# PSUM as one tile of eight named banks, read in pairs, in a kernel of a state-space convolution and a linear attention

## The chip, the cores and the metric

The kernel runs on one core of a Trainium2 chip. A core has a matrix engine (TensorE, PE in the profile, with its weight loads as PEld), a vector engine (VectorE, DVE), a scalar engine (ScalarE, ACT), GpSimd (POOL) and SyncE (SP), which here issues the DMA transfers. Each engine takes its own instructions in the order in which the program gives them, and waits on semaphores for the others. The metric is the time of one execution on the device, in microseconds (us); of several runs the median is taken.

## The reference

Two independent branches whose outputs stand side by side, 2048 x 1152 in fp32.

```python
def _A_ref(u, log_A_real, A_imag, C_real, C_imag, log_dt, D_skip):   # L=2048, D=576, N=128
    dt = jnp.exp(log_dt)
    A = -jnp.exp(log_A_real) + 1j * A_imag
    C = (C_real + 1j * C_imag) * dt[:, None]
    P = jnp.exp((A * dt[:, None])[:, :, None] * pos[None, None, :])
    K = 2.0 * jnp.einsum("dn,dnl->dl", C, P).real
    ...
    y = jnp.fft.irfft(Uf * Kf[None, :, :], L2)[:, :, :L]   # causal convolution of u with K
    ...
    return y + u * D_skip[None, None, :]

def _B_ref(x, wqkv, w_phi, wo):        # S=2048, D=576, 32 heads of 18
    ...
    q, k, v = qkv[0], qkv[1], qkv[2]   # of x @ wqkv
    pq = jnp.einsum("bhsd,hdf->bhsf", q, w_phi)
    pk = jnp.einsum("bhsd,hdf->bhsf", k, w_phi)
    phi_q = jnp.concatenate([_softmax(pq, axis=-1), _softmax(-pq, axis=-1)], axis=-1)
    phi_k = jnp.concatenate([_softmax(pk, axis=-1), _softmax(-pk, axis=-1)], axis=-1)
    kv = jnp.einsum("bhsf,bhsd->bhfd", phi_k, v)
    z  = jnp.einsum("bhsf->bhf", phi_k)
    num = jnp.einsum("bhqf,bhfd->bhqd", phi_q, kv)
    den = jnp.einsum("bhqf,bhf->bhq", phi_q, z)[..., None] + 1e-6
    o = num / den
    return (lambda x, *d: x.transpose(*d))(o, 0, 2, 1, 3).reshape(B, S, D) @ wo
```

## The kernel before

**How it is put together.** `body` does not issue instructions itself. It records some 3000 operations with `Plan.op`: each with its engine, the buffers that it reads and writes, and a function that issues it. A copy with engine `"any"`, and some other operations, have a second engine (`copy`, L265, and `tt`, L273). The order in which all are issued is written out by hand in the string `ORDER`, a list of operation numbers: an `x` behind a number puts that operation on its second engine, and a colon with a number puts so many filler matmuls on zeros ahead of it (`emit`, L194 to L207). So the order on each engine's queue, and on SP's for the transfers, is this string's. `Buf` objects get their memory when the first operation that uses them is issued, from pools with a fixed number of buffers by tag (L256 to L259). All PSUM buffers have the tag `ps`, of which there are 8, one bank (512 fp32 of each partition) each.

**Attention.** Weights of keys and queries are first multiplied by `w_phi` (`fold`, L311). Every gemm takes fp32 numbers as a high and a low part (`hi`, `lo`; fp32r), so one output of 128 rows is 14 matmuls that add up in one bank (`gemm`, from L372). There are 16 tiles of 128 rows. `key_tile` (L434) makes keys and values, 1152 columns, in three gemms of 378, 378 and 396 columns, in the banks `pa`, `pb` and `pc`; `pb` holds the end of the keys and the start of the values. `softmax` (L393) reads the keys from PSUM in two parts, 21 and 11 heads: for each a maximum and a minimum over a head (L400, L401), the addition of the maximum (L282) and a small sum (L403), all on DVE; after that one exponential for both signs on ACT (L408), sums on POOL (L411) and DVE (L412), and the scaling. Values are copied beside ones (`v1`), in two copies. 32 small matmuls of heads then add to `kvt`, one bank that stays taken through the key stage. `query_tile` (L495) makes queries in two gemms of 288 columns (`gemm_halves`, L385), takes `softmax` in two parts of 16 heads, transposes it through PSUM (`turn`, L504), multiplies by the key-value sums and divides (`divide`, L518), transposes again, and multiplies by `wo` in two gemms of 288 columns, copied out by two copies (`ot`).

**Convolution.** The FFT is done by matmuls in two steps with transfers through DRAM between them. `u_first` (L576) does the first step for the input, four banks of 288 columns, four copies to `zi`. The filter is made in 18 pairs of groups (`phases`, `waves`, `group`): `params` (L647) computes for each of 6 blocks of 96 columns, in a chain of 96-wide DVE and ACT operations (L659 and L666 are its helpers), the angles' integer phases `pi`; POOL builds the phases, ACT takes sines, PE and ACT the exponentials of the sizes (L762), DVE multiplies them (L768 to L773), PE sums over states. `k_first` (L787) with `first` (L564) does the first FFT step of the filter. `product` (L827, 16 of them) does the second step of both, multiplies (L282, `ac`), and goes the first step back; `last` (L905, 16) does the last one and writes the output. Each of these writes 288-column results to two or four banks, and copies each bank out by itself (`us`, `zo`, `yo`).

**The order around.** Key tiles are first, with the input's first steps; the groups run from then to about three quarters of the time, with queries and later products beside them; products, queries and last steps fill the end.

Of the kernel before, what the change touches and what calls it, by code (L numbers as in the profile page):

```python
# [11 lines left out]
I32 = mybir.dt.int32  # L12
# [130 lines left out]
class Buf:  # L143


    def __init__(self, tag, shape, dt):
        self.tag, self.shape, self.dt = tag, shape, dt
        self.writers, self.readers, self.left, self.end, self.t = [], [], 0, 0.0, None
# [9 lines left out]
class Plan:  # L158
# [14 lines left out]
    def buf(self, tag, shape, dt=F32):  # L173
        return Buf(tag, shape, dt)
# [19 lines left out]
    def emit(self, k, o, eng, fill=0):  # L194
        for b in o[4]:
            if b.t is None:
                b.t = self.pools[b.tag].tile(b.shape, b.dt, name=b.tag, tag=b.tag)
        if fill:
            b, (rows, cols) = o[11], o[10]
            t = b.t  # L200
# [8 lines left out]
    def run(self):  # L209

        seen = set()
        for word in ORDER.split():
            word, _, fill = word.partition(":")
            k = int(word.rstrip("x"))
# [4 lines left out]
            self.emit(k, o, o[12][0] if word[-1] == "x" else o[0], int(fill or 0))  # L219
# [25 lines left out]
def body(tc, nc, i, out, ctx):  # L245
# [10 lines left out]
    tags({1: "zero ident w1 w3 hp quarter dsk kvb fT wh wl ks E sel dt th cre cim ax ay mx mn ld ldc",  # L256
          2: "v1 o ot pi mg ff ub kb zo us2 ac yo zi", 3: "e fk x9", 4: "cs", 7: "small"})
    tags({8: "ps"}, space=PSUM)
# [52 lines left out]
    def fold(w_t, w, done, stage, after):  # L311
# [4 lines left out]
        def block(g, c, cs):  # L316
            wt, pa, pb = B(stage[g], [128, 640]), B("ps", [128, 4, 126]), B("ps", [128, 126])
            op("sp", c_dma(c * 2560), lambda: sp.dma_start(wt.t[:c], w_t[cs, :]), w=[wt])

            def f():  # L320
                for k in range(4):
                    mm(pa.t[:, k, :c], wt.t[:c, k * 128:k * 128 + 128], phiw.t[:c, g, :c])
            op("pe", 4 * 222, f, r=[wt, phiw], w=[pa], with_=[hi, lo])

            op("pe", 222, lambda: mm(pb.t[:, :c], wt.t[:c, 512:640], phiw.t[:c, g, :c]), r=[wt, phiw], w=[pb], with_=[hi, lo])
            a, b = (lambda x: x.t[:, 0:4, cs]), (lambda x: x.t[:, 4, cs])
            for x, ps, n in ((a, (lambda: pa.t[:, :, :c]), 4 * c), (b, (lambda: pb.t[:, :c]), c)):
                src, half = pa if x is a else pb, Mark()
                op("act", c_act(n), lambda x=x, ps=ps: act.activation(x(hi), ps(), AF.Copy), r=[src], w=[done[g], half], with_=[hi])
                op("dve", c_dve(n), lambda x=x, ps=ps: dve.tensor_tensor(x(lo), ps(), x(hi).bitcast(F32), op=ALU.subtract),  # L330
                   r=[src, half], w=[done[g]], with_=[hi, lo])
# [6 lines left out]
    def whole(src, w, done, stage, eng):  # L338
        hi, lo = w

        def third(c):
            wi, half = B(stage[c], [128, 5, 192]), Mark()
            cs = slice(D + 192 * c, D + 192 * c + 192)
# [49 lines left out]
    def softmax(parts, total=False):  # L393

        rg, sm, e = B("small", [128, 32]), B("small", [128, 32, 2]), B("e", [128, 2, H, DH])

        def part(p, hs, v):
            m = hs.stop - hs.start
            ends = B("small", [128, m, 2])
            op("dve", c_dve(DH * m), lambda: dve.tensor_reduce(ends.t[:, :, 0], v(), axis=AX.X, op=ALU.max, negate=True), r=[p], w=[ends])  # L400
            op("dve", c_dve(DH * m), lambda: dve.tensor_reduce(ends.t[:, :, 1], v(), axis=AX.X, op=ALU.min), r=[p], w=[ends])  # L401
            tt("dve", lambda: e.t[:, 0, hs, :], v, lambda: ends.t[:, :, 0:1].to_broadcast([128, m, DH]), ALU.add, [p, ends], [e], DH * m)
            op("dve", c_dve(2 * m), lambda: dve.tensor_reduce(rg.t[:, hs], ends.t, axis=AX.X, op=ALU.add), r=[ends], w=[rg])  # L403
        for p in parts:
            part(*p)
# [28 lines left out]
    def key_tile(t):  # L434
# [3 lines left out]
        pa, pb, pc = B("ps", [128, 378]), B("ps", [128, 378]), B("ps", [128, 396])  # L438
        by_head = lambda ap: ap.rearrange("p (h f) -> p h f", f=DH)
# [4 lines left out]
        e = softmax([(pa, slice(0, 21), lambda: by_head(pa.t)), (pb, slice(21, 32), lambda: by_head(pb.t[:, 0:198]))])  # L444
# [3 lines left out]
        copy("any", lambda: v1.t[:, 0:10, 0:18], lambda: by_head(pb.t[:, 198:378]), [pb], [v1], 180)  # L448
        copy("any", lambda: v1.t[:, 10:32, 0:18], lambda: by_head(pc.t), [pc], [v1], 396)
# [45 lines left out]
    def query_tile(t):  # L495
# [3 lines left out]
        e = softmax([(ps[c], slice(16 * c, 16 * c + 16), lambda c=c: ps[c].t.rearrange("p (h f) -> p h f", f=DH)) for c in range(2)], True)  # L499
# [4 lines left out]
        def turn(j0, n):  # L504
# [6 lines left out]
            op("pe", 110 * n, f, r=[e, ident], w=[tp], with_=[fT], busy=0.5)  # L511
# [37 lines left out]
        for c, cs in enumerate(halves):  # L549
# [499 lines left out]
```

## Time and profile before

| | us |
|---|---|
| median of 3 runs | 576.01 (573.24 to 577.25) |
| the profiled execution | 574.2 |
| its span, first to last instruction | 572.4 |

The profile is of that one execution. "Busy" is the time in which an engine worked on instructions; a matmul's time runs to the end of its pipeline, so neighbouring matmuls overlap, and PE's busy time holds short stalls. A row with "idle before" tells how long the engine stood still ahead of these instructions, and what ended that. The slices below are 1/40 of the span each, in tenths busy.

```profile
PE   7998799999999999998999999999999999999996
PEld 6998689888977777887887666867878866667884
DVE  5999779989989999999999999999876689866642
ACT  4775857788678989798699968788744334232332
POOL 0736589977778676982569755887311244112110
PEclk7999899999999999999999999999999999999999
DMA  8957432252857685717755758985568899998587
```

### The profile page before, as it was taken

Reading aid. Unit: us, or ns where it says so; the run is one execution under the profiler, and the core shown is the slowest. Engines: PE = TensorE matmul, PEld = TensorE weight load, DVE = VectorE, ACT = ScalarE, POOL = GpSimd, SP = SyncE. Lnnn points to the kernel's source line nnn. Section 1 sums busy time; section 2 is a strip of 40 time slices with the busy share of each in tenths; the row PEclk is TensorE's granted clock in tenths of the full one; section 3 lists DMA queues with packets and bytes.
Section 4 is the critical chain, followed back from the end, with each engine's and each line's share of the span. In section 5 each row is a group of like instructions: output and inputs, shape, how many; then the busy total and the mean of one; then the engine's idle time right before and its main releaser. Section 6 shows DMA issues by size and latency. Waiting matters only on the chain.

```text
span 572.4 us, 18462 instructions
## 1 busy us (share of the span) xinstructions
PE 542.3 (95%) x7526; PEld 444.1 (78%) x7526; DVE 491.0 (86%) x1059; ACT 383.6 (67%) x656; POOL 316.6 (55%) x454
## 2 busy tenths in 40 slices
PE   7998799999999999998999999999999999999996
PEld 6998689888977777887887666867878866667884
DVE  5999779989989999999999999999876689866642
ACT  4775857788678989798699968788744334232332
POOL 0736589977778676982569755887311244112110
PEclk7999899999999999999999999999999999999999
DMA  8957432252857685717755758985568899998587
GB/s 249 302 172 254 159 145 88 86 187 91 277 150 217 205 264 159 208 44 184 216 190 156 239 153 233 309 255 188 169 246 228 228 288 282 286 277 280 172 283 208
DMA packets 91314, 119.22 MB, mean 208 GB/s; under 512 B 9826, under 2 KB 73186, under 8 KB 91230
## 3 DMA queue, kind: packets, MB, share of 16 engines
q1 hardware_dynamic: 91230, 118.04, 67.1%
q8 instruction: 59, 0.97, 0.7%
q14 instruction: 25, 0.20, 0.1%
HBM read 68.76 MB, written 49.26 MB: 206 GB/s over the span
## 4 chain that ended last, share of the span: by engine, by line
PE 48%; DVE 28%; DMA 8%; ACT 7%; issue 4%; POOL 3%; SPq 1%; DVEq 0%; POOLq 0%; ACTq 0%
PE ps L263 44%; DVE cs L768 2%; DVE E L769 2%; PE ps L510 2%; DMA kb<-dram 2%; POOL cs L720 2%; DVE zi L268 2%; DVE e L282 2%; DMA zi<-dram 1%; DVE small L401 1%; DVE small L412 1%; DVE small L400 1%; DVE E L773 1%; ACT ps L762 1%; DVE x L278 1%
## 5 line engine op out<-in xcount | busy, mean ns | idle before, releaser
L263 PE MATMUL ps<-wh,x 128*128 128x288 f32 (+2 forms) x1008 | 241.0, 320 | 2.5 <-DVE zi L268 1.0
L263 PEld LDWEIGHTS ps<-wh,x 128*128 128x128 f32 x1008 | 173.9, 189 | 13.9 <-issue 3.4
L263 PE MATMUL ps<-wl,x 128*128 128x288 f32 (+2 forms) x560 | 175.4, 314 | 0.0
L720 POOL TENSOR_TENSOR cs<-cs,pi 128x32 int32<-128x32 int32 (+4 forms) x180 | 112.0, 627 | 8.7
L263 PEld LDWEIGHTS ps<-wl,x 128*128 128x128 f32 x560 | 106.0, 189 | 0.7
L762 ACT ACTIVATE ps<-ps 128x512 f32<-128x512 f32 x108 | 59.9, 588 | 12.2 <-PE ps L263 11.9
L411 POOL TENSOR_TENSOR o<-e 128x576 f32<-128x576 f32 x32 | 42.1, 1316 | 35.5 <-ACT e L408 35.5
L278 POOL TENSOR_TENSOR e<-e,small 128x576 f32<-128x576 f32 (+1 forms) x27 | 44.9, 1662 | 28.1 <-DVE small L282 23.1
L278 POOL TENSOR_TENSOR ac<-ac 128x288 f32<-128x288 f32 x43 | 34.5, 820 | 45.4 <-DVE ac L282 37.2
L278 POOL TENSOR_TENSOR e<-small,e 128x576 f32<-128x576 f32 x24 | 28.5, 1189 | 42.8 <-DVE small L403 29.3
L768 DVE TENSOR_TENSOR cs<-ps,cs 128x1024 f32<-128x1024 f32 x36 | 43.6, 1212 | 7.4 <-ACT ps L762 7.3
L282 DVE TENSOR_TENSOR ac<-us,ps 128x576 f32<-128x576 f32 x64 | 45.2, 745 | 5.3 <-PE ps L263 4.9
L263 PEld LDWEIGHTS ps<-kvb,fT 126*128 126x128 f32 (+1 forms) x320 | 38.4, 188 | 8.1 <-issue 2.2
L769 DVE TENSOR_TENSOR E<-ps,cs 128x1024 f32<-128x1024 f32 x36 | 43.6, 1211 | 1.0 <-ACT ps L762 1.0
L408 ACT ACTIVATE e<-e 128x1152 f32<-128x1152 f32 x32 | 37.3, 1168 | 9.0 <-POOL e L278 5.3
L263 PEld LDWEIGHTS ps<-E,cs 128*32 128x32 f32 x2304 | 34.3, 110 | 11.4 <-issue 4.4
L263 PE MATMUL ps<-kvb,fT 126*128 126x133 f32 (+1 forms) x320 | 41.5, 280 | 1.2 <-ACT zi L268 1.2
L263 PE MATMUL ps<-sel,mg 128*128 128x512 f32 x108 | 38.1, 444 | 3.8 <-ACT sel L271 2.5
L263 PE MATMUL ps<-E,cs 128*32 128x64 f32 x2304 | 40.2, 221 | 0.9 <-DVE E L769 0.4
L268 ACT ACTIVATE zi<-ps 128x288 f32<-128x288 f32 x77 | 28.0, 411 | 17.2 <-PE ps L263 12.0
L263 PE MATMUL ps<-kb,fk 128*64 128x288 f32 x256 | 36.4, 416 | 2.4 <-DMA kb<-dram 1.2
L744 ACT ACTIVATE cs<-cs 128x1040 f32<-128x1040 int32 x36 | 38.3, 1063 | 0.4 <-POOL cs L739 0.2
(141 smaller groups left out, 1039.7 us busy)
## 6 DMA issues: line engine op xcount, KB each, us to landing
xd<-x SPq DMA_DIRECT2D x16, 576.0 KB
dram<-zi SPq DMA_DIRECT2D x16, 576.0 KB
dram<-zi SPq DMA_DIRECT2D x32, 288.0 KB
x<-xd SPq DMA_DIRECT2D x16, 576.0 KB
kb<-dram SPq DMA_DIRECT2D x32, 288.0 KB
ub<-dram SPq DMA_DIRECT2D x32, 288.0 KB
dram<-zo SPq DMA_DIRECT2D x32, 288.0 KB
zi<-dram SPq DMA_DIRECT2D x16, 576.0 KB
```

The source lines that it names most:

```text
L263: pe.matmul(o, l, r, start=start, stop=stop, skip_group_check=skip)
L268: op(("act", "dve"), (c_act(n), c_dve(n)), lambda e: act.activation(dst(), src(), AF.Copy) if e == "act" else dve.tensor_copy(dst(), src() ...
L278: op(eng, [c_dve(n[0]) if e == "dve" else c_pool(n[1]) for e in eng], lambda e: (dve if e == "dve" else pool).tensor_tensor(dst(), a(), b( ...
L282: op(eng, c_dve(n) if eng == "dve" else c_pool(n), lambda: e.tensor_tensor(dst(), a(), b(), op=alu), r=r, w=w, lock=eng == "pool" or not a ...
L408: op("act", c_act(1152) + 40, lambda: act.activation(e.t, e.t, AF.Exp), r=[e], w=[e], table="exp")
L411: op("pool", c_pool(470), lambda: pool.tensor_tensor(pair.t, e.t[:, :, :, 0:9], e.t[:, :, :, 9:18], op=ALU.add), r=[e], w=[pair], lock=True)
L510: pe.transpose(tp.t[0:m, j - j0, :], e.t[:, sign, 7 * g:7 * g + GRP[g], :].rearrange("p h f -> p (h f)"), ident.t)
L720: op("pool", c_pool(2 * n * W), lambda n=n, j=j: pool.tensor_tensor(x()[:, :, :, n:2 * n], x()[:, :, :, 0:n], pi.t[:, j:j + 2, gs].bitcast ...
L744: act.activation(cs.t[:, 1], cs.t[:, 1].bitcast(I32), AF.Sin, scale=TURN)
L762: op("act", c_act(512), lambda: act.activation(ps.t, ps.t, AF.Exp), r=[ps], w=[ps], table="exp")
L768: op("dve", c_dve(64 * W), lambda: dve.tensor_tensor(F(), both(M.t), F(), op=ALU.mult), r=[M, cs], w=[cs])
L769: op("dve", c_dve(64 * W), lambda: dve.tensor_tensor(E.t[:, :, :, 32:64], both(up.t), cs.t[:, :, :, 0:32], op=ALU.mult), r=[up, cs], w=[E])
```

## The change

PSUM becomes one tile of eight banks. A buffer asks for one bank or two neighbouring ones, and the order string names the first bank of each buffer that an operation takes (`@` and digits) in place of a pool that hands them out. Results that stood in two banks become one buffer over two, and one operation reads both:

- keys are one pair of 2 x 288 columns and values another, four gemms of 288 in place of three; `softmax` reads the keys, or queries, in one part;
- `v1`, `ot`, `zi`, `us`, `zo` and `yo` are copied in pairs, and `ac` is one multiplication of 4 x 288 in place of two;
- `params` runs its chain on 192 columns, for two blocks at a time, and only the last steps on each block;
- `yo` uses the buffers of `ot` (three instead of two each), `mx` that of `ax`;
- `fold` puts its five results into one pair;
- operations are renumbered (2575 in place of 2973) and the order string is new, with 38 filler matmuls where there were 62, and other choices of the second engine in places.

```diff
+    def banks(self, b, k):
+        p, *dims = b.shape
+        t = self.psum[0:p, k:k + b.banks]
...
-    def emit(self, k, o, eng, fill=0):
+    def emit(self, k, o, eng, fill=0, at=""):
+        at = iter(at)
         for b in o[4]:
-            if b.t is None:
+            if b.t is None and b.tag == "ps":
+                self.banks(b, int(next(at)))
+            elif b.t is None:
                 b.t = self.pools[b.tag].tile(b.shape, b.dt, name=b.tag, tag=b.tag)
...
-          2: "v1 o ot pi mg ff ub kb zo us2 ac yo zi", 3: "e fk x9", 4: "cs", 7: "small"})
-    tags({8: "ps"}, space=PSUM)
+          2: "v1 o pi mg ff ub kb zo us2 ac zi", 3: "e fk x9 ot", 4: "cs", 7: "small"})
+    pl.psum = ctx.enter_context(tc.tile_pool(name="banks", bufs=1, space=PSUM)).tile([128, 8, 512], F32, name="psum")
...
     def gemm_halves(x, w, done, c0):
-        r = []
-        for cs, need in zip(halves, done):
-            ps = B("ps", [128, 288])
-            gemm(x, w, need, ps, lambda ps=ps: ps.t, slice(c0 + cs.start, c0 + cs.stop))
-            r.append(ps)
-        return r
+        ps = B("ps", [128, 2, 288], banks=2)
+        for c, (cs, need) in enumerate(zip(halves, done)):
+            gemm(x, w, need, ps, lambda c=c: ps.t[:, c], slice(c0 + cs.start, c0 + cs.stop))
+        return ps
...
-        def part(p, hs, v):
-            m = hs.stop - hs.start
-            ends = B("small", [128, m, 2])
-            op("dve", c_dve(DH * m), lambda: dve.tensor_reduce(ends.t[:, :, 0], v(), axis=AX.X, op=ALU.max, negate=True), r=[p], w=[ends])
...
-        for p in parts:
-            part(*p)
+        ends, two = B("small", [128, H, 2]), lambda ap: ap.rearrange("p (c h) -> p c h", c=2)
+        op("dve", c_dve(D), lambda: dve.tensor_reduce(two(ends.t[:, :, 0]), v(), axis=AX.X, op=ALU.max, negate=True), r=[p], w=[ends])
+        op("dve", c_dve(D), lambda: dve.tensor_reduce(two(ends.t[:, :, 1]), v(), axis=AX.X, op=ALU.min), r=[p], w=[ends])
...
-        pa, pb, pc = B("ps", [128, 378]), B("ps", [128, 378]), B("ps", [128, 396])
-        gemm(x, wkv, have_k[0:3], pa, lambda: pa.t, slice(0, 378))
-        gemm(x, wkv, have_k[3:5] + have_v[0:1], pb, lambda: pb.t, slice(378, 756))
-        gemm(x, wkv, have_v, pc, lambda: pc.t, slice(756, 1152))
+        pk = gemm_halves(x, wkv, (have_k[0:3], have_k[2:5]), 0)
+        pc = gemm_halves(x, wkv, (have_v[0:2], have_v[1:3]), D)
...
-        copy("any", lambda: v1.t[:, 0:10, 0:18], lambda: by_head(pb.t[:, 198:378]), [pb], [v1], 180)
-        copy("any", lambda: v1.t[:, 10:32, 0:18], lambda: by_head(pc.t), [pc], [v1], 396)
+        copy("any", lambda: v1.t[:, :, 0:18].rearrange("p (c h) f -> p c h f", c=2), lambda: by_head(pc), [pc], [v1], D)
...
-        for m in range(4):
-            copy("any", lambda m=m: o.t[:, m], lambda m=m: ps[m].t, [ps[m]], [o], HD)
+        for m in range(2):
+            copy("any", lambda m=m: o.t[:, 2 * m:2 * m + 2], lambda m=m: ps[m].t, [ps[m]], [o], D)
...
-            for part in range(2):
-                tt("dve", lambda part=part: ac.t[:, 2 * part:2 * part + 2], lambda: us[r].t, lambda part=part: pk[part].t[:, None].to_broadcast([128, 2, HD]),
-                   ALU.mult, [us[r], pk[part]], [ac], 2 * HD)
+            tt("dve", lambda: ac.t.rearrange("p (x y) n -> p x y n", x=2), lambda: us[r].t[:, None].to_broadcast([128, 2, 2, HD]),
+               lambda: pk.t[:, :, None].to_broadcast([128, 2, 2, HD]), ALU.mult, [us[r], pk], [ac], 4 * HD)
...
     def params(blk):
-        cs = slice(blk * BW, blk * BW + BW)
+        P2 = 2 * BW
+        cs = slice(blk * BW, blk * BW + P2)
...
+        def block(pi, x):
+            fx = B("ot", [128, 4, BW])
+            for k, m in ((0, 1), (1, -64), (3, -32)):
+                op("dve", c_dve(BW, True), lambda k=k, m=m: dve.tensor_scalar(
+                    pi.t[:, k], th.t[:, x], float(np.float32(1 / (2 * math.pi))) * m, None, op0=ALU.mult), r=[th], w=[pi], lock=True)
+            tt("dve", lambda: pi.t[:, 2], lambda: at.t[:, x], lambda: mn.t[:, x], ALU.add, [at, mn], [pi], BW)
...
+        for n, pi in enumerate(pis):
+            pl.at("par", blk + n)
+            block(pi, slice(n * BW, n * BW + BW))
+        return pis
```

`first`, `product`, `last` and the copy of `ot` change as `u_first` does here: two buffers of two banks (`last`: one) for four (two) of one bank, and one copy for each pair.

More of the change, by code (lines that the diff above doesn't have):

```diff
@@ L171, in step, with buf @@
         self.part = name
-    def buf(self, tag, shape, dt=F32):
-        return Buf(tag, shape, dt)
+    def buf(self, tag, shape, dt=F32, banks=1):
+        return Buf(tag, shape, dt, banks)
+    def banks(self, b, k):
+        p, *dims = b.shape
+        t = self.psum[0:p, k:k + b.banks]
+        if b.banks > 1:
+            t, dims = t, dims[1:]
+        else:
+            t = t.rearrange("p b n -> p (b n)")
+        n = 1
+        for d in dims:
+            n *= d
+        t = t[..., 0:n]
+        if len(dims) > 1:
+            names = "abcd"[:len(dims)]
+            lead = "p z" if b.banks > 1 else "p"
+            t = t.rearrange(f"{lead} ({' '.join(names)}) -> {lead} {' '.join(names)}", **dict(zip(names[1:], dims[1:])))
+        b.t = t
     def op(self, eng, cost, fn, r=(), w=(), with_=(), table=None, busy=1.0, lock=False, mode=(128, 128), add=None):
@@ L199, in emit @@
             b, (rows, cols) = o[11], o[10]
-            t = b.t
+            t = b.t[:, 0] if b.banks > 1 else b.t
             while len(t.shape) > 2:
@@ L341, in third @@
         def third(c):
-            wi, half = B(stage[c], [128, 5, 192]), Mark()
-            cs = slice(D + 192 * c, D + 192 * c + 192)
+            cs, half = slice(D + 192 * c, D + 192 * c + 192), Mark()
+            wi = B(stage[c], [128, 5, 192])
             load_rows(wi, src, slice(192 * c, 192 * c + 192), 192)
@@ L498, in query_tile @@
         pl.step("q1")
-        e = softmax([(ps[c], slice(16 * c, 16 * c + 16), lambda c=c: ps[c].t.rearrange("p (h f) -> p h f", f=DH)) for c in range(2)], True)
+        e = softmax(ps, lambda: ps.t.rearrange("p c (h f) -> p c h f", f=DH), True)
         pl.step("q3")
@@ L548, in query_tile @@
         ot = B("ot", [128, D])
-        for c, cs in enumerate(halves):
-            copy("any", lambda c=c, cs=cs: ot.t[:, cs], lambda c=c: po[c].t, [po[c]], [ot], 288)
+        copy("any", lambda: ot.t.rearrange("p (c n) -> p c n", c=2), lambda: po.t, [po], [ot], D)
         op("sp", c_dma(128 * 2304, 2304), lambda: sp.dma_start(out[t * 128:t * 128 + 128, 576:1152], ot.t), r=[ot])
@@ L564, in first @@
     def first(b, src, n, o, dst, view):
-        ps = [B("ps", [128, n]) for _ in range(4)]
+        ps = [B("ps", [128, 2, n], banks=2) for _ in range(2)]
         def f():
@@ L578, in u_first @@
         op("sp", c_dma(128 * 2304), lambda: sp.dma_start(us.t, i["u"][:, D * k:D * k + D]), w=[us])
-        ps = [B("ps", [128, HD]) for _ in range(4)]
+        ps = [B("ps", [128, 2, HD], banks=2) for _ in range(2)]
         pl.step("u1")
@@ L841, in product @@
         us = [B("us2", [128, 2, HD]) for _ in range(2)]
-        pu, begun = [B("ps", [128, HD]) for _ in range(4)], Mark()
+        pu, begun = [B("ps", [128, 2, HD], banks=2) for _ in range(2)], Mark()
         def f():
@@ L862, in times @@
             op("sp", c_dma(128 * 2304, 1152), lambda: sp.dma_start(kb.t, blk()), r=[kd[half]], w=[kb])
-            pk = [B("ps", [128, HD]) for _ in range(2)]
+            pk = B("ps", [128, 2, HD], banks=2)
             def f():
@@ L884, in product @@
         pl.step("p4")
-        pz, zo = [B("ps", [128, HD]) for _ in range(4)], [B("zo", [128, 2, HD]) for _ in range(2)]
+        pz, zo = [B("ps", [128, 2, HD], banks=2) for _ in range(2)], [B("zo", [128, 2, HD]) for _ in range(2)]
         def back():
@@ L890, in back @@
                     for r in range(2):
-                        mm(pz[c].t[64 * r:64 * r + 64], fi()[32 * c:32 * c + 32, r, part, :], acs[r].t[32 * c:32 * c + 32, 2 * part], part == 0, part == 1, True)
-        op("pe", 970, back, r=[ff, *acs], w=pz, with_=zo, mode=(32, 64))
-        for c in range(4):
-            j, par = divmod(c, 2)
-            copy("any", lambda c=c, j=j, par=par: zo[par].t[:, j], lambda c=c: pz[c].t, [pz[c]], [zo[par]], HD)
+                        mm(pz[c % 2].t[64 * r:64 * r + 64, c // 2], fi()[32 * c:32 * c + 32, r, part, :], acs[r].t[32 * c:32 * c + 32, 2 * part], part == 0, part == 1, True)
+        op("pe", 970, back, r=[ff, *acs], w=pz, mode=(32, 64))
+        for par in range(2):
+            copy("any", lambda par=par: zo[par].t, lambda par=par: pz[par].t, [pz[par]], [zo[par]], D)
         for par in range(2):
@@ L906, in last @@
         pl.at("last", 8 * half + cb // 4)
-        yo, zi = B("yo", [128, 2, HD]), B("zi", [128, 4, HD])
+        yo, zi = B("ot", [128, 2, HD]), B("zi", [128, 4, HD])
         op("sp", c_dma(128 * 4608), lambda: sp.dma_start(
             zi.t, zd[half].t.rearrange("q (r b) d -> (q r) b d", r=2)[:, cb:cb + 4]), r=[zd[half]], w=[zi])
-        ps = [B("ps", [128, HD]) for _ in range(2)]
+        ps = B("ps", [128, 2, HD], banks=2)
         pl.step("l1")
```

327 lines of the change are left out of this document (161 added, 166 removed), and 4 rows, old and new, of the table ORDER.

## The prediction

> **What bounds the kernel now.** I read the page's busy shares first, then the chain that ended last, then the windows view by stage, then the form-by-form groups for prices.
>
> ```profile
> span 572.4 us, 18462 instructions
> PE 542.3 (95%) x7526; PEld 444.1 (78%) x7526; DVE 491.0 (86%) x1059; ACT 383.6 (67%) x656; POOL 316.6 (55%) x454
> PE 48%; DVE 28%; DMA 8%; ACT 7%; issue 4%; POOL 3%; SPq 1%; DVEq 0%; POOLq 0%; ACTq 0%
> ...
> 57.00:115.00 58.00, 54.33 (x953) 49.30 (x939) 50.13 (x105) 41.98 (x64) 45.96 (x62) 0.97 0.35 118
> 115.00:150.00 35.00, 33.48 (x544) 30.07 (x543) 32.26 (x75) 31.05 (x46) 23.44 (x34) 1.00 0.46 158
> 150.00:250.00 100.00, 94.55 (x1514) 78.97 (x1512) 97.07 (x203) 82.14 (x129) 78.70 (x110) 1.00 0.65 196
> 250.00:350.00 100.00, 95.12 (x1466) 73.49 (x1468) 96.85 (x209) 84.87 (x151) 63.36 (x99) 1.00 0.64 183
> 350.00:400.00 50.00, 49.51 (x844) 36.22 (x836) 46.30 (x95) 40.30 (x67) 38.84 (x64) 1.00 0.80 251
> 400.00:450.00 50.00, 48.85 (x672) 40.98 (x671) 35.72 (x73) 27.46 (x54) 11.54 (x11) 1.00 0.74 218
> 450.00:500.00 50.00, 48.37 (x557) 34.93 (x556) 44.16 (x100) 18.32 (x41) 18.28 (x18) 1.00 0.91 274
> 500.00:560.00 60.00, 59.43 (x611) 45.76 (x610) 37.92 (x89) 20.33 (x50) 10.47 (x11) 1.00 0.81 252
> ```
>
> The window rows give start:end, length, then busy time (and count) of PE, weight loads, DVE, ACT and POOL, the granted clock, the DMA share and GB/s. PE alone looks like the bound, but two regimes stand side by side. From 115 to 350 us DVE is busy 32.26 + 97.07 + 96.85 = 226.2 of 235 us, fuller than PE (33.48 + 94.55 + 95.12 = 223.2), at a granted clock of 1.00. From 350 us on PE is at 97 to 99% and DVE falls to 63% by the end: there DVE work is cover. The chain agrees: 48% of it is PE, but 28% is DVE, that is 0.28 x 572.4 = 160 us, a third of all DVE work. So DVE time taken away is worth about a third of itself overall, and more in the middle.
>
> **The change, part by part.** First the prices, of one shape each: instructions, busy us, mean ns.
>
> ```profile
> L400 DVE TENSOR_REDUCE small<-ps 128x16 f32<-128x288 f32 x32 | 14.0, 441 | 0.0
> L400 DVE TENSOR_REDUCE small<-ps 128x21 f32<-128x378 f32 x16 | 8.5, 537 | 0.2 <-PE ps L263 0.2
> L400 DVE TENSOR_REDUCE small<-ps 128x11 f32<-128x198 f32 x16 | 5.7, 354 | 0.0
> L403 DVE TENSOR_REDUCE small<-small 128x16 f32<-128x32 f32 x32 | 5.5, 175 | 0.2
> L403 DVE TENSOR_REDUCE small<-small 128x21 f32<-128x42 f32 x16 | 3.0, 184 | 0.0
> L412 DVE TENSOR_REDUCE small<-o 128x64 f32<-128x576 f32 x32 | 23.5, 738 | 4.8 <-POOL o L411 4.8
> L282 DVE TENSOR_TENSOR ac<-us,ps 128x576 f32<-128x576 f32 x64 | 45.2, 745 | 5.3 <-PE ps L263 4.9 <-ACT us L268 0.3
> L768 DVE TENSOR_TENSOR cs<-ps,cs 128x1024 f32<-128x1024 f32 x36 | 43.6, 1212 | 7.4 <-ACT ps L762 7.3
> L268 DVE COPY zi<-ps 128x288 f32<-128x288 f32 x51 | 21.6, 440 | 4.8 <-PE ps L263 3.5 <-issue 1.2
> L268 ACT ACTIVATE zi<-ps 128x288 f32<-128x288 f32 x77 | 28.0, 411 | 17.2 <-PE ps L263 12.0 <-issue 3.7 <-ACT zi L268 0.9
> L762 ACT ACTIVATE ps<-ps 128x512 f32<-128x512 f32 x108 | 59.9, 588 | 12.2 <-PE ps L263 11.9
> ```
>
> On DVE 1024 against 576 elements is 1212 against 745 ns, 1.04 ns an element; of the 745 ns some 145 are thus what an operation costs whatever its size. On ACT (588 - 411)/224 = 0.79 ns an element: a 576-column copy is an estimated 640 ns against 2 x 411.
>
> Softmax, 32 tiles: the three reads of PSUM become one each of 576 columns, about 742 ns by the 738 and 745 rows. A key tile paid 537 + 354 = 891, a query tile 2 x 441 = 882; so 149 and 140 ns saved, three times a tile. The small sum over the ends (L403) becomes one of 64 elements, about 205 ns by its slope, against 2 x 175 or nearly as much: 140 saved. (3 x 149 + 140) x 16 + (3 x 140 + 140) x 16 = 9.4 + 9.0 = 18.4 us of DVE.
>
> Product: 64 multiplies of 745 ns become 32 of 1152 elements, 1212 + 128 x 1.04 = 1345: 145 x 32 = 4.6 us.
>
> Copies: `zi`, `us`, `zo`, `yo`, `ot` and `v1` leave in pairs. The new order string (an x behind a number puts an operation on its second engine) gives DVE 59 pairs in place of 124 halves: 124 x 0.445 - 59 x 0.745 = 11.2 us; the key values' copies go the other way by about 0.9. So 10.3 us of DVE. ACT gets 101 pairs for 196 halves: 196 x 0.411 - 101 x 0.64 = 16 us; with some `fT` and `ks` copies and two `abs` moved off it by the string, and half the parameter activations, about 25 us of ACT.
>
> ```profile
> L666 DVE TENSOR_SCALAR pi<-th x18: 195/202/2296, 10.4 to 333.6; 128x96 f32<-128x96 f32 x18
> L666 DVE TENSOR_SCALAR pi<-th 128x96 f32<-128x96 f32 x18 | 8.4, 470 | 0.0
> L282 DVE TENSOR_TENSOR dt<-dt,ay 128x96 f32<-128x96 f32 x18 | 5.9, 326 | 0.3
> L282 DVE TENSOR_TENSOR dt<-dt,ay x18: 242/254/1173, 10.8 to 333.8; 128x96 f32<-128x96 f32 x18
> L678 DVE RECIPROCAL dt<-dt x6: 740/742/748, 7.5 to 286.4; 128x96 f32<-128x96 f32 x6
> ```
>
> Parameters (the rows with slashes are minimum/median/maximum): of 50 DVE operations for two blocks 32 stay, so 7 tensor-scalar, 10 tensor-tensor and one reciprocal go, three times. The 96 further elements cost the survivors about 50, 100 and 600 ns. By the medians a pair saves 7 x (202 - 50) + 10 x (254 - 100) + 140 = 2.7 us; by the means, which hold the 2 us cases, 7 x 420 + 10 x 226 + 140 = 5.3 us. Three times: 8.2 to 16 us. I take 12, as the long cases come with an operation started, and fewer start.
>
> Flexible work moved by the string: DVE loses six `ac` sums and six halves of `x`, and takes six `fT`, four `ks` and a few softmax operations: about zero. POOL gains some 11 us. DVE in all: 18.4 + 4.6 + 10.3 + 12 = 45.3 us of 491.
>
> [...]
>
> What of it lies on the path: by the chain 160/491 = 0.327 of DVE, so 14.8 us. By the other count, the stage of 115 to 350 us loses 45.3/491 of its 226.2 us, 20.9, if nothing else binds; PE's idle time there is 235 - 223.2 = 11.8, what it can give up at least without being itself faster. 14.8 lies between, and I take it. ACT's share of the chain is 7%, 40 us of 383.6: 25 x 0.104 = 2.6. POOL 17 of 316.6: 11 x 0.054 = +0.6.
>
> PE itself:
>
> ```profile
> 118.69 0.51 PE L263 MATMUL ps<-wh,x 128*128 128x378 f32 x2
> 119.21 0.51 PE L263 MATMUL ps<-wh,x 128*128 128x378 f32 x2
> ...
> 305.06 0.30 PE L263 MATMUL ps<-wh,x 128*128 128x288 f32 x1
> 306.90 0.29 PE L263 MATMUL ps<-wh,x 128*128 128x288 f32 x1
> ```
>
> Fourteen matmuls of 288 columns start in 1.84 us, 131 ns apart; three of 378 in 0.52 us, 173 apart, so one of 396 is an estimated 181. A key tile's 14 x (173 + 173 + 181) = 7.38 us becomes 56 x 131 = 7.34: nothing, though 224 matmuls are added. The filler matmuls on zeros fall from 62 to 38. They stand where PE would wait anyway, so zero. Of the steps moved, the parameter loads are half as many DMAs on SP (12 for 24) and start earlier; the `yo` output uses the `ot` buffers, three for both. The rest of the order keeps its stages: key, groups, queries, products and queries with the last stage at the end, with the same number of DMAs for each.
>
> What the change adds is a longer hold of PSUM: an eviction waits until both banks are written, and frees both at its end. No such wait is in the trace; nearest are PE's waits for evictions (us in total, times, longest):
>
> ```profile
> PEld ps L263 <- DVE zi L268: 5.2, 10, 1.1
> PEld ps L263 <- DVE e L282: 2.9, 6, 0.9
> PEld ps L263 <- ACT zi L268: 2.5, 5, 1.5
> PEld ps L263 <- ACT us L268: 1.4, 4, 0.4
> ```
>
> If these 25 waits each grow by 745 - 440 = 0.3 us, that is +7.5; if freer engines end them, -12. I take +3, nearer to the first, since the same engines run and each operation is longer. Sum: -14.8 - 2.6 + 0.6 + 0 + 3 = -13.8 us. The profiled execution took 574.2 us (572.4 its span), 1.8 below the median of the three runs: 560.4 against it, 562 against 576.0.
>
> **The rivals.** *More comes out.* All 20.9 us of the middle, ACT's 2.6, and a part, 3, of the eviction waits: 576 - 26 = 550. For it: DVE at 97% for 200 us, and that a new order can use room which the chain of the old one does not show. Against it: PE has 11.8 us of visible idle time there, so the rest must come out of its short stalls.
>
> *PE hides it.* The freed DVE time turns into idle time before the same matmuls: 573, a gain of 3. For it: PE is at 95% over all and at 97 to 99% after 350 us, its matmul time does not shrink, and DMA is at 0.91 from 450 to 500 us. Against it: 28% of the chain is DVE.
>
> *PSUM runs short, and it is slower.* One bank holds the sums of keys and values through the key stage, so seven others give three pairs and one single; the single-bank uses (sizes, transposes, `divide`) break pairs up. There are 240 pair uses: 32 each of keys, values' or outputs' and queries' gemms, the first transforms and so on. If PE waits 0.3 us longer at each, 72 us; the net gain without the 3 us is 16.8, so 56 late pairs of 240 undo it and about 75 make it slower by over 1%. At 40% late, 29 us: 576 - 17 + 29 = 588. For it: before, the first of two halves leaves while the second is computed. Against it: an eviction of 0.745 us stands against 1.84 us for one gemm half. [...] In the same rival belongs that one tile for all of PSUM makes operations wait for banks that they don't touch, in which case pairs don't do what they say.
>
> **How the numbers follow.** Forecast 0.50 (562), more 0.20 (550), hidden 0.18 (573), short of PSUM 0.12 (588). About 1% is what a measurement of this kernel can tell from no change: faster 0.70, within 0.18, slower 0.12. The range leaves out the slower rival and the tip of the second: low 546, from 576 less 20.9, 2.6 and half of the 12 us of waits; high 576. The likeliest case's own range is 555 to 569.
>
> **What would show it.** Right: DVE's busy time near 446, with 576-column reduces near 742, 1152-element multiplies near 1345 and copies near 745 and 640 (ACT); its share from 115 us on falls well below 97% while PE's busy share rises above 95%; DVE's part of the chain falls under 28%. Wrong: PE's waits for evictions over 20 us, or idle time before paired gemms, speaks for the third rival; DVE idle for PE with the span unchanged, for the second. Parameter operations above 0.5 us each would take the 12 us back. The prediction fails outright if paired operations cost more than twice one half.

## The result, and the profile after

| | before | after |
|---|---|---|
| median of 4 runs each, us | 575.13 (573.24 to 577.25) | 561.31 (560.45 to 561.75) |
| the profiled execution, us | 574.2 | 561.75 |
| its span, us | 572.4 | 560.0 |

The ratio is 0.9756, 95% interval 0.9715 to 0.9796: 2.4% faster, 13.8 us. (The runs of this comparison include the three that were shown before.) Of all runs in this document one, 581.29 us among the ten of the last experiment, fell in a slower state; without it their median is 573.89 us.

First the page after the change: busy time of each engine, and the shares of the chain that ended last.

```profile
PE 533.4 (95%) x7726; PEld 444.5 (79%) x7726; DVE 462.3 (83%) x775; ACT 370.9 (66%) x530; POOL 325.5 (58%) x465
PE 74%; DMA 10%; DVE 9%; issue 3%; SPq 2%; ACT 2%; ACTq 0%; DVEq 0%
```

Against before, DVE issues 284 fewer instructions and is busy 28.7 us less (491.0 to 462.3), and its part of the chain falls from 28% to 9%. PE is busy 8.9 us less although it runs 200 more matmuls; its busy time holds stalls, and they must have shrunk, as the gemms' matmuls of 288 columns start as far apart as before, a median of 133 ns in both. The rest of the 12.4 us of span is PE's idle time, 30.1 to 26.6 us. The weight loads' busy time did not move (444.1 and 444.5 us).

The windows by stage, with the columns of before (start:end, length, then busy time and count of PE, weight loads, DVE, ACT, POOL, then granted clock, DMA share, GB/s):

```profile
115.00:150.00 35.00, 33.29 (x634) 29.66 (x627) 29.67 (x46) 29.21 (x38) 28.04 (x44) 1.00 0.52 170
150.00:250.00 100.00, 96.95 (x1650) 84.16 (x1648) 86.69 (x149) 82.79 (x121) 81.15 (x114) 1.00 0.62 194
250.00:350.00 100.00, 99.09 (x1572) 76.75 (x1569) 93.02 (x163) 83.70 (x122) 67.82 (x111) 1.00 0.71 204
350.00:400.00 50.00, 49.18 (x735) 39.13 (x742) 44.84 (x67) 37.93 (x53) 35.78 (x53) 1.00 0.75 230
```

From 150 to 350 us DVE was at 97% and PE at 95% before; now DVE is at 87 and 93%, PE at 97 and 99%. The order is new, so the same stretch need not hold the same work. Most of this is what the prediction had named as the signs of its being right. One sign did not come: DVE's busy time was to fall by 45.3 us, to near 446, and it fell by 28.7, to 462.3. The durations of DVE's instructions fell by more than forecast, from 558.7 to 504.4 us in sum; why the two differ is shown below. Then the groups by form (instructions, busy us, mean ns, idle before):

```profile
L303 DVE TENSOR_TENSOR ac<-us,psum 128x1152 f32<-128x1152 f32 x32 | 42.2, 1348 | 8.0 <-PE psum L284 4.1 <-ACT zo L289 3.5
L415 DVE TENSOR_REDUCE small<-psum 128x32 f32<-128x576 f32 x32 | 23.9, 746 | 2.3 <-PE psum L284 2.2
L414 DVE TENSOR_REDUCE small<-psum 128x32 f32<-128x576 f32 x32 | 23.8, 743 | 6.5 <-PE psum L284 6.5
L289 DVE COPY zi<-psum 128x576 f32<-128x576 f32 x25 | 18.6, 750 | 6.6 <-PE psum L284 4.3 <-DMA dram<-zi 1.9 <-DMA out_dram<-ot 0.2
L685 DVE RECIPROCAL ax<-ax 128x192 f32<-128x192 f32 x3 | 4.0, 1349 | 0.1
L289 ACT ACTIVATE zi<-psum 128x576 f32<-128x576 f32 x39 | 24.5, 649 | 18.2 <-PE psum L284 13.5 <-DMA dram<-zi 4.5
```

The prices are those forecast to within 1.5%: 743 and 746 for 742, 1348 for 1345, 750 and 649 for 745 and 640. So the number, the prices and the signs came out, but for DVE's busy time. Whether the cause did is another question, and the experiments answer it: mostly not.

### The profile page after: what moved, and what is told of

Its sections match the earlier page's. It is cut to its first block, busy times and chain, and to the rows that moved or that the text cites. A ratio compares the mean times of both kernels' runs of the same rounds, so it can differ in the third digit from the quotient of the medians.

```text
span 560.0 us, 18413 instructions
## 1 busy us (share of the span) xinstructions
PE 533.4 (95%) x7726; PEld 444.5 (79%) x7726; DVE 462.3 (83%) x775; ACT 370.9 (66%) x530; POOL 325.5 (58%) x465
## 4 chain that ended last, share of the span: by engine, by line
PE 74%; DMA 10%; DVE 9%; issue 3%; SPq 2%; ACT 2%; ACTq 0%; DVEq 0%
PE psum L284 70%; DMA out_dram<-ot 3%; PE psum L520 2%; PE psum L548 1%; DMA e<-in_wkT_dram 1%; DMA dram<-zo 1%; DMA kb<-dram 1%; DMA dram<-zi 1%; DMA fk<-in_fk_dram 1%; DVE e L299 1%; DMA ff<-in_ff_dram 1%; SPq L937 1%; DVE x L299 1%; DMA mg<-gd 1%; DVE E L785 1%
## 5 line engine op out<-in xcount | busy, mean ns | idle before, releaser
L284 PE MATMUL psum<-wh,x 128*128 128x288 f32 x1152 | 244.5, 300 | 3.0 <-ACT e L421 1.8
L284 PEld LDWEIGHTS psum<-wh,x 128*128 128x128 f32 x1152 | 188.8, 189 | 11.5 <-issue 4.3
L284 PE MATMUL psum<-wl,x 128*128 128x288 f32 x640 | 187.2, 295 | 0.0
L284 PEld LDWEIGHTS psum<-wl,x 128*128 128x128 f32 x640 | 121.0, 189 | 0.9
L424 POOL TENSOR_TENSOR o<-e 128x576 f32<-128x576 f32 x32 | 43.1, 1349 | 63.7 <-ACT e L421 63.6
L778 ACT ACTIVATE psum<-psum 128x512 f32<-128x512 f32 x108 | 59.3, 586 | 18.2 <-PE psum L284 17.7
L299 POOL TENSOR_TENSOR e<-e,small 128x1152 f32<-128x1152 f32 (+1 forms) x26 | 44.7, 1722 | 19.3 <-DVE small L303 12.9
L784 DVE TENSOR_TENSOR cs<-psum,cs 128x1024 f32<-128x1024 f32 x36 | 43.7, 1214 | 8.0 <-ACT psum L778 7.9
L303 DVE TENSOR_TENSOR ac<-us,psum 128x1152 f32<-128x1152 f32 x32 | 42.2, 1348 | 8.0 <-PE psum L284 4.1
L785 DVE TENSOR_TENSOR E<-psum,cs 128x1024 f32<-128x1024 f32 x36 | 43.6, 1212 | 3.3 <-ACT psum L778 2.9
L284 PEld LDWEIGHTS psum<-E,cs 128*32 128x32 f32 x2304 | 34.1, 110 | 12.4 <-issue 7.9
L284 PE MATMUL psum<-kvb,fT 126*128 126x133 f32 (+1 forms) x320 | 41.6, 279 | 0.2 <-ACT fT L289 0.2
```

What stands on the lines that cost most here:

```text
L284: pe.matmul(o, l, r, start=start, stop=stop, skip_group_check=skip)
L299: op(eng, [c_dve(n[0]) if e == "dve" else c_pool(n[1]) for e in eng], lambda e: (dve if e == "dve" else pool).tensor_tensor(dst(), a(), b( ...
L303: op(eng, c_dve(n) if eng == "dve" else c_pool(n), lambda: e.tensor_tensor(dst(), a(), b(), op=alu), r=r, w=w, lock=eng == "pool" or not a ...
L424: op("pool", c_pool(470), lambda: pool.tensor_tensor(pair.t, e.t[:, :, :, 0:9], e.t[:, :, :, 9:18], op=ALU.add), r=[e], w=[pair], lock=True)
L778: op("act", c_act(512), lambda: act.activation(ps.t, ps.t, AF.Exp), r=[ps], w=[ps], table="exp")
L784: op("dve", c_dve(64 * W), lambda: dve.tensor_tensor(F(), both(M.t), F(), op=ALU.mult), r=[M, cs], w=[cs])
```

## The experiments

All were timed in three rounds beside the kernel before, whose median in the four comparisons was 574.6, 574.9, 573.5 and 573.6 us. The line numbers of an edited kernel are shifted by its edits.

### Is it the merged operations? Taking the merging back

**Everything in halves.** The new order, its banks and its gemms stay, and a pair of banks is still named and taken as one; each merged operation is issued as two halves, one behind the other.

```diff
-        op("dve", c_dve(D), lambda: dve.tensor_reduce(two(ends.t[:, :, 1]), v(), axis=AX.X, op=ALU.min), r=[p], w=[ends])
+        op("dve", c_dve(D), lambda: [dve.tensor_reduce(
+            two(ends.t[:, :, 1])[:, c], v()[:, c], axis=AX.X, op=ALU.min) for c in range(2)], r=[p], w=[ends])
...
-            tt("dve", lambda: dst.t, lambda: x.t, lambda: y.t, alu, [x, y], [dst], P2)
+            op("dve", c_dve(P2), lambda: [dve.tensor_tensor(dst.t[:, z], x.t[:, z], y.t[:, z], op=alu) for z in two], r=[x, y], w=[dst], lock=True)
```

> The changed kernel with its order, banks and gemms, but every merged read, copy, multiplication and parameter operation issued as its two halves again, one behind the other at the same place. Theory of relief (the gain is DVE and ACT time that merging takes away): most of the 14 us come back, 570 to 577 us, DVE's share of the chain is over 20% again. Rival (the gain is the new order and the named banks, merging is hidden by PE): 561 to 565 us.

Measured: 562.37 us (559.55 to 563.76), ratio 0.9799 (0.9748 to 0.985). Without any merging the new order is as fast as with it, 1.1 us apart, well inside the intervals. Its page, and two of its windows:

```profile
PE 533.3 (96%) x7726; PEld 445.0 (80%) x7726; DVE 476.6 (85%) x1056; ACT 380.9 (68%) x651; POOL 324.6 (58%) x465
PE 71%; DMA 13%; DVE 8%; SPq 3%; issue 2%; POOL 1%; ACT 1%; DVEq 0%; ACTq 0%
```

```profile
150.00:250.00 100.00, 97.80 (x1662) 84.66 (x1660) 90.07 (x199) 85.36 (x140) 82.75 (x115) 1.00 0.62 195
250.00:350.00 100.00, 99.95 (x1569) 77.98 (x1569) 96.07 (x214) 85.58 (x150) 67.93 (x112) 1.00 0.71 208
```

The number of DVE's instructions is back (1056, before 1059) and its busy time half back; PE's busy time and DVE's share of the chain stay where the change put them. So the signs that I had named, PE above 95% in the middle and DVE's part of the chain under 28%, come with the order and its banks, not with the merging. They didn't test the reason.

**One kind in halves.** The copies alone (1), the reads of `softmax` and `ac` alone (2), the parameters alone (3), each with its part of the edit above; for the copies it is

```diff
-            op(("act", "dve"), (c_act(n), c_dve(n)), lambda e: act.activation(dst(), src(), AF.Copy) if e == "act" else dve.tensor_copy(
-                dst(), src()), r=r, w=w)
+            def one(e, d, s):
+                act.activation(d, s, AF.Copy) if e == "act" else dve.tensor_copy(d, s)
+            op(("act", "dve"), (c_act(n), c_dve(n)), lambda e: [one(e, dst()[:, c], src()[:, c]) for c in range(2)] if r[0].banks > 1 else one(
+                e, dst(), src()), r=r, w=w)
```

> Only the copies out of PSUM (v1, zi, us, zo, ot, yo) in halves again, on ACT and DVE. Relief: a share by DVE time, some 3 us, 563 to 567. Rival: within 2 us of the changed kernel.

> Only DVE's softmax reads and the multiplications of the products in halves again. Relief: the largest part, 5 us, 564 to 569. Rival: within 2 us of the changed kernel.

> Only the parameter chain as two of 96 columns again, each operation twice. Relief: some 3 us, 563 to 567, as by durations it is DVE's largest part. Rival: within 2 us of the changed kernel.

| in halves | us | ratio (interval) | DVE busy, instructions |
|---|---|---|---|
| copies | 557.16 (555.54 to 557.43) | 0.9694 (0.9653 to 0.9735) | 463.3, x842 |
| reads, `ac` | 561.04 (558.61 to 563.74) | 0.9769 (0.9714 to 0.9824) | 467.9, x935 |
| parameters | 562.78 (559.45 to 564.48) | 0.9791 (0.9739 to 0.9843) | 466.4, x829 |

The reads and the parameters make no difference that can be told. The copies are better apart, which neither theory had foretold: all four runs lie below all four of the changed kernel, with ACT's busy time 9.2 us higher (380.1 against 370.9). Of all kernels here that have their whole work this is the fastest, ahead of before and after. The intervals of the two ratios still touch, and with all other operations in halves as well nothing is left of the gain (562.4). Why was not isolated, but the trace shows what halves can give: the first may leave while PE still works on the second bank. Of the 22 pairs of `ot` copies on ACT six have their halves 1.2 to 2.6 us apart from start to start, where back to back it is 0.3. The widest pair (start, duration):

```profile
417.22 0.41 ACT L290 ACTIVATE ot<-psum 128x288 f32<-128x288 f32 x1
419.83 0.41 ACT L290 ACTIVATE ot<-psum 128x288 f32<-128x288 f32 x1 [2.20 <-PE psum L284]
```

So taking the merging back has two effects, more time on the engines and an earlier start. The 1.1 us of the kernel with everything in halves is what is left of both; it doesn't say that each is nothing.

**What an instruction saved is worth.** The groups of DVE sum to 545.1 us in the kernel with everything in halves, 504.4 after: 40.7 us for 281 instructions, a mean of 145 ns, the fixed cost that the prediction worked out from the rows. DVE's busy time differs by only 476.6 - 462.3 = 14.3 us, 51 ns each. The timeline of before shows why (start, duration):

```profile
118.70 0.35 DVE L401 TENSOR_REDUCE small<-ps 128x11 f32<-128x198 f32 x1
118.97 0.68 DVE L773 SCALAR_TENSOR_TENSOR E<-ps,cs 128x512 f32<-128x512 f32 x1
119.57 0.74 DVE L412 TENSOR_REDUCE small<-o 128x64 f32<-128x576 f32 x1
```

The reduce of 0.35 us ends at 119.05, and the next has started at 118.97; that one ends at 119.65, after the third's start at 119.57. Neighbours overlap by some 0.08 us. Over the whole kernel before, the durations sum to 558.7 us in 491.0 us of busy time. In the kernel with everything in halves the second half of a softmax addition (L420) starts 365 ns after the first (median of 32) and the two take 812 ns, where one over both banks takes 745: 67 ns for an instruction, not 145. So the durations overstated here what DVE gained by an instruction less; the distance from start to start gave it.

### Was DVE, or PE, what bound it?

**Less DVE work.** The minimum over each head reads 1 of its 18 values, in the kernel before and in the one after.

```diff
-            op("dve", c_dve(DH * m), lambda: dve.tensor_reduce(ends.t[:, :, 1], v(), axis=AX.X, op=ALU.min), r=[p], w=[ends])
+            op("dve", c_dve(DH * m), lambda: dve.tensor_reduce(ends.t[:, :, 1], v()[:, :, 0:1], axis=AX.X, op=ALU.min), r=[p], w=[ends])
```

> The kernel before, with the minimum over a head taken over 1 of its 18 values (that part of the softmax's shift is left out): some 18 us less DVE time by durations, PE's work as it was. Theory that DVE bounds a part of the kernel before (28% of its chain): 5 to 8 us faster, 567 to 570. Rival (PE alone bounds it): within 2 us of the kernel before.

> The changed kernel with the same left out: some 18 us less DVE time. Theory that the change took DVE off the path (9% of the chain): 1 to 3 us faster, 558 to 560. Rival (DVE still bounds as much as before): 5 to 8 us faster.

Measured: before with less, 569.01 us (566.92 to 572.34), ratio 0.9898 (0.9826 to 0.997), with DVE's busy time 14.5 us lower (476.5); after with less, 559.15 us (554.37 to 560.68), ratio 0.9706 (0.9641 to 0.9771), with 15.7 us lower (446.6). In the old order some 6 us of 14.5 came out of the time, 0.40 of the relief, about the third that the chain gave. In the new one 2 of 15.7, within the intervals. So DVE time did count before, and the prediction was right there. In the new order it counts for less by the medians, but each of the two gains is uncertain by some 4 us, so this pair alone doesn't show it. A wider step helps: between the new order in halves and the new order with less lie 30.0 us of DVE's busy time (476.6 and 446.6) and 3.2 us of time, where a third would be 10. By the ratios' intervals it could be 0.6 to 10.1, so a third lies at the very edge. What the order and its banks give is not DVE's busy time: the kernel with everything in halves has DVE as busy as the old order with less (476.6 against 476.5) and is 6.6 us faster.

**Less PE work.** Two of the 14 matmuls of each gemm with fp32 parts are taken out, 33.6 us of PE before by their distances, 33.5 after.

```diff
-                mm(p, x.t[:, k, :], wl.t[:, k, cs], False, False)
+                if k % 2:
+                    mm(p, x.t[:, k, :], wl.t[:, k, cs], False, False)
```

> The kernel before with 2 of the 14 matmuls of every gemm left out (products of the high part of x with the low part of the weights, for two of the row blocks): 33.6 us of PE by starts 131 to 181 ns apart. Theory that DVE binds in the middle: only the part outside it comes out, 15 to 22 us faster, 553 to 560. Rival (PE alone bounds): 28 to 34 us faster.

> The changed kernel with the same matmuls left out: 33.5 us of PE. Theory that PE is its bound nearly everywhere (74% of the chain): 24 to 32 us faster, 529 to 537. Rival (bounds as before, shared with DVE): 15 to 22 us faster.

Measured: before with less, 567.75 us (564.75 to 572.49), ratio 0.9881 (0.9794 to 0.9968); after with less, 543.98 us (543.47 to 545.05), ratio 0.9459 (0.9416 to 0.9502). Of the same 33.6 us, 7 came out of the time before, less than either theory had given, and 17 after, in the rival's range. The kernel before with less PE work, and its two windows with a lower granted clock (the column before the last two):

```profile
PE 520.3 (92%) x7302; PEld 417.2 (74%) x7302; DVE 489.3 (87%) x1059; ACT 382.5 (68%) x656; POOL 314.6 (56%) x454
PE 35%; DVE 34%; DMA 11%; ACT 7%; POOL 6%; issue 5%; SPq 1%; POOLq 0%; DVEq 0%; ACTq 0%
...
57.00:115.00 58.00, 51.63 (x893) 45.97 (x881) 49.12 (x101) 39.86 (x61) 43.88 (x62) 0.91 0.35 118
115.00:150.00 35.00, 34.22 (x534) 30.09 (x534) 33.52 (x76) 32.28 (x49) 23.79 (x34) 0.95 0.45 155
```

PE was at 95% before, and yet with 33.6 us of its matmuls gone its busy time fell by only 22.0 us, and its idle time grew by 15.3 (30.1 to 45.4). The other 11.6 us stayed in what counts as busy, as stalls or as slower matmuls. Slower ones are part of it: in the kernel before, matmuls of 396 columns start 0.33 us apart where the granted clock was 0.50 (67.5 to 69.1 us) and 0.18 where it was 1.00 (72.0 to 73.5). In the two windows the clock was 0.91 and 0.95, before it was 0.97 and 1.00, which is an estimated 5 us of PE at full clock (0.06 x 58 + 0.05 x 35). All four runs of this kernel were granted 0.976 to 0.983 on average, those of the kernel before 0.983 to 0.991, and those of the changed kernel with less 0.986 to 0.995. So the 7 us might be up to 12 at an equal clock; no run tells. Neither engine alone bound the kernel before: 14.5 us less DVE gave 6, 33.6 us less PE gave 7 to 12, and PE's waits for DVE and ACT grew from 67.9 to 91.7 us with its own work less. They waited for each other. That PE is nearer to being the bound after the change is likely by the 17 us, but with the clock between them not shown; half of its relief is lost there too.

PE's busy share tells none of this: it is 95% before and 95% after, with 7 and 17 us measured for the same relief. The weight loads' 78% and 79% do not tell the two apart either.

### The order, or its banks?

**The old order with other banks.** Nothing is merged and the order is the old one; only PSUM is one tile of eight banks, and a buffer gets the bank that has been free longest in the order of issue.

```diff
+        for b in new:
+            self.bank(b, self.free.pop(0))
...
+                if not b.left:
+                    self.free.append(b.bank)
...
-    tags({8: "ps"}, space=PSUM)
+    pl.psum = ctx.enter_context(tc.tile_pool(name="banks", bufs=1, space=PSUM)).tile([128, 8, 512], F32, name="psum")
```

> The kernel before, nothing merged, its order as it was, but PSUM as one tile of eight banks; each buffer takes the bank that has been free longest when its first operation is issued. With the merged operations worth nothing in the new order, two theories are left. Banks (the gain is that a buffer takes a bank that is free, and not the pool's next): 563 to 569 us. Order (the gain is the new sequence of operations on each engine): 573 to 577 us.

Measured: 569.52 us (567.46 to 575.91, 10 runs), ratio 0.9943 (0.9913 to 0.9974). A small gain, 3 to 4 us, from the choice of banks alone, just outside the range of the theory of banks. One tile for all of PSUM made nothing slower here, which the prediction had held possible.

**The old order, merged.** The same, with 176 pairs of operations joined in one, issued where the first half stood; `params` and the key gemms are as before.

```diff
+            join(None, len(pl.ops) - 2, len(pl.ops) - 1, lambda e, r=r: one(e, us[r].t, pl.pair(pu[2 * r], pu[2 * r + 1])))
```

> As the run before, and 176 pairs merged in the old order: copies to zi, us, zo and yo and the multiplications of the products, each pair at the place of its first half. Order theory with DVE binding in the old order: 3 to 6 us faster than that run, as 18 us less DVE time gave 5.8 us in the kernel before. Order theory with merging worth nothing anywhere: within 2 us of that run, or slower, as two halves on two engines become one on one.

**The new order, merged, without the names.** The changed kernel, but a buffer's banks are those that have been free longest, neighbours where there are any.

```diff
-        t = self.psum[0:p, k:k + b.banks]
+            near = [(max(free.index(x), free.index(x + 1)), x) for x in free if x + 1 in free]
+            at = [min(near)[1], min(near)[1] + 1] if near else sorted(free[:2])
+            t = self.psum[0:p, at[0]:at[1] + 1:at[1] - at[0]]
```

> The changed kernel with its merged operations and its order, but the named banks ignored: each buffer takes what has been free longest, pairs two neighbours where there are such, else any two. Banks theory: the gain goes, 568 to 576 us. Order theory: within 2 us of the changed kernel's 561.3.

Measured: the old order merged, 600.75 us (598.5 to 602.51), ratio 1.0452 (1.0415 to 1.0489), 31 us above the same order in halves; the new order without its names, 601.99 us (600.18 to 602.21), ratio 1.048 (1.0453 to 1.0507), 41 us above the changed kernel; neither loss had been foretold at this size. In the second of them DVE has even less to do than in the changed kernel (460.8 us), and PE waits for evictions (weight loads' waits: us in total, times, longest):

```profile
PEld psum L303 <- DVE ac L322: 8.7, 8, 2.1
PEld psum L303 <- ACT zi L308: 8.2, 12, 1.7
PEld psum L303 <- DVE e L322: 7.6, 6, 3.3
PEld psum L303 <- DVE zi L308: 6.5, 6, 2.5
```

Two things are mixed in these two. A pair waits for both of its banks and frees them late (an `ac` over both takes 1348 ns, over one 748). And where no neighbours were free a pair lay in banks apart (25 of 176 pairs in the first, 16 of 250 in the second). Whether an access to such a pair made operations wait for work on the banks between is not shown by any run, nor how much of the 31 and 41 us that would be; the next run has no such access. Of the 41 us an estimated 6 are clock, 0.01 of 602: the second kernel was granted 0.976 to 0.985, the kernel before beside it 0.986 to 0.991.

**The new order in halves, without the names.** The first experiment's kernel with the last edit: no instruction reads two banks.

> The new order with every merged operation issued as two halves, as in the first experiment of this study (562.4 us), but the bank of each PSUM buffer is the one that has been free longest, as before the change, and the names in the order are ignored. No instruction reads two banks at once, so an access across banks can't make one wait for a bank in between. If the names carry the gain (an order that works only where the bank of each buffer has been chosen with it), 570 us or more, with PE's waits for evictions several times those of the first experiment. If the order carries it, and the 602 us of the merged version came from reads across banks that lie apart, within 3 us of 562.4.

Measured: 574.36 us (571.89 to 581.29, 10 runs), ratio 1.0034 (0.9993 to 1.0075). That is the time of before, and 12 us above the first experiment, from which it differs by the banks alone. (Its rule is that of the old order with other banks, not that of the pool before the change.) It is also 28 us below the merged kernel by the same rule. So merging, which cost nothing with the names, costs 28 us without them, whatever the pairs in banks apart cost and the lower clock included. The waits of the weight loads, first with the names, then without:

```profile
PEld psum L284 <- DVE e L420: 3.7, 4, 2.7
PEld psum L284 <- ACT fT L290: 2.2, 4, 1.0
PEld psum L284 <- ACT zi L290: 2.0, 6, 0.4
PEld psum L284 <- DVE o L305: 1.8, 4, 0.5
```

```profile
PEld psum L303 <- DVE e L439: 6.2, 8, 2.7
PEld psum L303 <- ACT fT L309: 4.3, 7, 1.2
PEld psum L303 <- ACT zi L309: 3.9, 8, 1.7
PEld psum L303 <- DVE ac L912: 3.3, 5, 1.0
PEld psum L303 <- DVE o L324: 2.5, 4, 1.2
```

Each of the four that both show is longer, by 0.7 to 2.5 us, though the names change no instruction, no order and no duration (DVE's sum to 545.0 and 544.1 us), and the granted clock is the same within 0.01. The theory of the names had foretold 570 us or more and it is 574.4; that they grow to several times was too much, these four grow by 39 to 95%. The new order without its names, by this one rule, is worth nothing (574.4, and 569.5 for the old one by the same rule, there with single banks in place of pairs).

### One view that follows the time

The rows of the waits view for PE and its weight loads that a DVE or ACT operation ended, summed for each kernel that has all its matmuls:

| kernel | DVE busy, us | PE busy, us | PE's waits for DVE and ACT, us | profiled execution, us |
|---|---|---|---|---|
| after, less DVE | 446.6 | 532.9 | 42.9 | 560.7 |
| after, copies in halves | 463.3 | 532.6 | 44.0 | 555.5 |
| after | 462.3 | 533.4 | 44.7 | 561.8 |
| after, reads and `ac` in halves | 467.9 | 534.6 | 44.8 | 559.5 |
| after, parameters in halves | 466.4 | 535.5 | 46.8 | 559.5 |
| after, all in halves | 476.6 | 533.3 | 50.7 | 559.6 |
| before, less DVE | 476.5 | 539.6 | 59.5 | 569.2 |
| old order, other banks | 490.9 | 543.4 | 63.7 | 575.9 |
| before | 491.0 | 542.3 | 67.9 | 574.2 |
| new order in halves, no names | 477.9 | 537.9 | 68.1 | 571.9 |
| old order, merged | 485.3 | 555.4 | 100.0 | 602.5 |
| new order, merged, no names | 460.8 | 548.3 | 110.8 | 602.2 |

The kernels fall in three groups, by waits and by time alike: 43 to 51 us of waits at 556 to 562, 60 to 68 at 569 to 576, and 100 and more at 602. Inside a group the order isn't kept. DVE's busy time doesn't follow: it is 462.3 us after and 460.8 in the last row, 40 us slower. PE's busy time, which holds its short stalls, goes with the time as well; the waits tell besides whom PE waits for. Each row is one execution; that of the old order with other banks was the slowest of its ten, 6.4 us above their median. The waits of PE and of its weight loads can overlap, so the sum is a scale, not a time.

## Why the prediction was right, and where not

It said 562.0 us and 561.3 was measured, inside the likeliest case's own range. That the number fits so closely is luck: the term that makes up nearly all of it is worth about nothing in the kernel as built, and what carries the change was put at zero. Of its steps:

- *DVE binds the middle, and a third of what is saved comes out.* For the old order this held (6 us for 14.5 of busy time). For the kernel with the new order the runs give less (2 for 15.7, 3 for 30.0), with a third at the edge of the intervals, and the change brought both at once. The step that failed is the price: a third, a share of busy time in one order, was applied to durations and across a change of order, where merging alone gave 1.1 us in place of 14.8.
- *45.3 us of DVE, 14.8 of them on the path.* The durations were about right, and merging alone took 40.7 us of them. As engine time it was 14.3, and in the time 1.1 us net, inside the noise. This term, nearly all of the forecast gain, was not where the gain came from. Of the merging alone the result is that of the rival called "PE hides it"; that PE hid it is not shown, as halves also start earlier.
- *Copies: 10.3 us of DVE, 25 of ACT.* ACT's busy time fell by 12.7 (24.1 by durations), and the kernel that gives the merged copies back is some 4 us faster, so here the sign was wrong.
- *Parameters 12 us.* The kernel that issues them in halves has 10.4 us more by durations, 4.1 us more busy time on DVE, and takes 1.5 us more, within the intervals.
- *PE itself, and its order: zero.* The matmuls' distances were right. But the order and the names were costed as nothing beyond what the merging does to them, and they carry the change: with the names and without any merging 562.4, without the names 574.4.
- *A longer hold of PSUM: +3.* The four rows that the prediction shows, 12.0 us before, are 6.7 after (`zi` on DVE 0.9, `e` 2.0, `zi` on ACT 2.4, `us` 1.4), and all of PE's waits for DVE and ACT fell from 67.9 to 44.7 us. So the sign was wrong, and mostly it was not freer engines that ended them: in the new order in halves, with the banks named and DVE as busy as in the same kernel without names the sum is 50.7 in place of 68.1.
- *The rival in which PSUM runs short* came true without the names. With banks by a rule the merged new order takes 602.0 us, with 110.8 us of PE's waits for DVE and ACT, where 588 us had been worked out for it, though how much of that the pairs in banks apart cost is not known. Its other half, that one tile makes operations wait for banks that they don't touch, is refuted for buffers of one bank by the old order with other banks, which got faster; for pairs in banks apart it is open.

The choice of banks counts by 12 us for the same instructions in the same order (562.4 and 574.4 us). Nor did pairs lose where their banks were named: 561.3 us in the new order, against 562.4 with the same in halves.

Why the names beat the rule is not shown by a run of its own, and no other rule was tried. A reading that fits: "free longest" goes by the order in which instructions were issued, and the engines don't run in step, so the bank whose last reader was issued first need not be the first to be free; names can follow the times. Nor was it tried to give the old order names of its own, so how much the order adds to them is open.

## What to carry to other kernels

A share of the chain prices a small edit in the order at hand (it gave 6 us for 14.5 of DVE here) and need not hold across a new order; when a change bundles an order with cheaper operations, issue the cheap operations in their old form within the new order before believing in them. Where two engines wait for each other, sum PE's waits by what ends them: that went with the time here when DVE's busy time did not. Look at the granted clock before reading a small relief as a wait. Count an instruction saved by the distance from start to start, not by its duration (51 against 145 ns here), and choose the bank of each PSUM buffer with the same care as the order (12 us here).

## What was not expected of the hardware

DVE's instructions overlap at their ends, by some 0.08 us in the timeline above: 558.7 us of durations in 491.0 us of busy time before, and 51 ns of busy time for an instruction saved whose fixed part is 145 ns by duration. The engine's time for that part is about half of it or less (51 ns over all 281, of which 86 read no PSUM, and 67 for the softmax additions, which do).
